# Loading the first expert's weights into the lower half of their slot instead of through three shared buffers

## The chip, the core and the metric

The kernel runs on one core of one Trainium2 chip. The metric is the device time of one execution in microseconds. The kernel before takes 1584.69 us, the median of three runs (1584.22 to 1586.04).

## What is computed

Three layers follow each other. An attention without a score matrix (softmax over the features of q, softmax over the sequence of k, products of k and v per head) gives 4608 rows of 512 features. Each row goes through one of eight experts (the one with the largest router value), and the result of that layer through the two best of eight other experts, chosen with noise. Cut to what matters:

```
q_s = softmax(q, features);  k_s = softmax(k, sequence)      # 8 batches, 8 heads, 576 x 64
x   = q_s @ (k_s^T @ v)                                      # 4608 x 512

# layer 1, one expert per row
e   = argmax(x @ w_gate);  g = softmax(x @ w_gate)[e]
x2  = g * (relu(x @ w1[e]) @ w2[e])                          # w1: 512 x 1024, w2: 1024 x 512

# layer 2, two experts per row
noisy = x2 @ w_gate2 + log1p(exp(x2 @ w_noise)) * noise
out   = sum over the top two: softmax weight * (relu(x2 @ w1'[e]) @ w2'[e])
```

## The kernel before

Rows are routed to experts in lists, and an expert's rows are worked off in blocks of 128. A block multiplies its rows by w1 and w2 of its expert. To keep float32 precision TensorE multiplies in three products: each operand x is split into a high part, hi = x rounded to TensorE's reduced float32 type, and a low part, lo = x - hi; a product is hi*hi + lo*hi + hi*lo.

One expert's weights fill a *slot* of on-chip memory: 16384 float32 columns on 128 partitions, the hi parts in columns 0 to 8191 and the lo parts in columns 8192 to 16383. Two slots lie side by side in a hand-placed tensor `W` (line 1694), declared in the reduced type. While the first stage runs, the second slot's bytes hold the attention's inputs, through a second hand-placed tensor `A` (line 1696). Because W and A share memory, the code declares with `apart` (line 168) that instructions on the first slot ("W0") and on A don't depend on each other.

The program has a first stage, and then loops over blocks. The first stage is one list of steps (class `Plan`): each step names its engine, a cost, what it reads and writes, and a lag after which its result can be used. A list scheduler orders these steps by the length of what still hangs on them, tries several settings, keeps the order with the shortest planned end, and issues the instructions of every engine in that order. On the chip each engine, and the SyncE queue (SP) that issues nearly all transfers, works its instructions strictly in that order, and waits where a dependency found by the framework is not yet met. The stage holds:

- the attention over eight batches and 36 tiles of 128 rows (`query`, line 1455): load q (SP), maximum (VectorE), transposes (TensorE), exponential (ACT), product (TensorE), copy to a row buffer `xrow` (ACT, line 1306), scaling (VectorE or GpSimd, line 1322), store to memory (SP, line 1327). There are five row buffers;
- the router of layer 1 in five groups of tiles (`gates`, line 1479): VectorE steps, two products on TensorE (lines 1393 and 1394), and one indirect store per tile by GpSimd that enters the rows in the lists (line 1420);
- the weights of the *first expert*, that of row 0, which is known after the first group (`first_parts`, line 810). They come in eight parts of 1024 columns, 512 KB each. Parts 0 to 3 hold w1, parts 4 to 7 hold w2. For each part there is a load by SP (line 151), a cast to the hi part by ACT (line 208) and a subtraction raw - hi by VectorE (line 215);
- two blocks of that expert (`first_blocks`, line 829), whose rows are gathered by GpSimd (line 271) and transposed by TensorE (line 257). The second half of a block's second product (`y1`) needs parts 6 and 7. The second block also runs the router of layer 2. During it the rows of the first loop block are gathered, for which all lists must be complete.

The eight parts pass through three buffers, in the order (1, 0, 2, 1, 0, 2, 0, 2): buffer 0 is `raw0`, buffer 1 is `h`, where the blocks keep their hidden values, and buffer 2 lies in `x2`, where they keep results. A load into a buffer waits until cast and subtraction of the part before it in that buffer are done. For the plan the buffers are named ("raw", 0) to ("raw", 2); the activations that write `h` and `x2r`, and a store of zero rows from `x2r` (line 1745), name them too.

Of the kernel before, what the change touches and what calls it, by code (L numbers as in the profile page):

```python
# [10 lines left out]
F32 = mybir.dt.float32  # L11
# [11 lines left out]
N, D, E, F = B * S, H * HD, 8, 1024  # L23
# [6 lines left out]
K = 4  # L30
SL = 8192 // K
HL = SL // 2
SLOT = 16384
# [114 lines left out]
def load_part(nc, z, raw, i, c0=0, n=SL):  # L148

    a = z.wall[i] if isinstance(i, int) else z.wall[ds(i, 1)].rearrange("o p x -> (o p) x")  # L150
    return nc.sync.dma_start(raw, a[:, c0:c0 + n])
# [25 lines left out]
class Parts:  # L177

    def __init__(self, nc, z, i, ahi, alo, halves, raws, mm=None, apo=None):
        self.nc, self.z, self.i, self.ahi, self.alo, self.apo, self.mm = nc, z, i, ahi, alo, apo, mm
        self.to_load, self.halves, self.raws = list(halves), list(halves), list(raws)
        self.use, self.his, self.los = {}, {}, []

    def load(self, n):
        for _ in range(min(n, len(self.to_load))):
            k = self.to_load.pop(0)
            self.use[k] = self.raws.pop(0)
            load_part(self.nc, self.z, self.use[k], self.i + k // 2, k % 2 * HL, HL)  # L190

    def free(self, i, others, late):
        for y in others:
# [18 lines left out]
    def lo(self, k, pool=False):  # L212
        z = self.z
        eng, o = (self.nc.gpsimd, self.apo) if pool else (self.nc.vector, self.alo)
        i = eng.tensor_tensor(cols(z, o + 8192 + k * HL, HL), self.use[k], f32(cols(z, o + k * HL, HL)),
                              op=OP.subtract)
        self.free(i, [h for n, h in self.his.items() if n != k] + [y for y in self.los if y.ins.engine != i.ins.engine],
                  self.late(k))
        self.los.append(i)
        self.raws.append(self.use.pop(k))  # L220

    def go(self, n):
        for _ in range(n):
# [586 lines left out]
def first_parts(nc, z, P, regs):  # L810

    add, parts = P.add, []
    seq = (1, 0, 2, 1, 0, 2, 0, 2)
    raws = [(z.raws[0], z.h, z.x2[:, 0:HL])[i] for i in seq]

    def load():
        if not parts:
            parts.append(Parts(nc, z, regs[0] * K, 0, 0, range(2 * K), raws, apo=0))
        parts[0].load(1)

    for k in range(2 * K):
        raw = ("raw", seq[k])
        add("SP", 1.46, load, ["expert"], [raw, "parts' turn"], 1.0)
        add("ACT", 0.95, lambda k=k: parts[0].hi(k), [raw], [("hi", k)])
        pool = k in POOL_LO
        add("POOL" if pool else "DVE", 2.0 if pool else 1.14, lambda k=k, pool=pool: parts[0].lo(k, pool), [raw, ("hi", k)], [("lo", k), "parts' end"])


def first_blocks(tc, z, pipe, P, wreg, late):
# [21 lines left out]
    def block(i):  # L851
        b = bs[i]
        mm(b.m0, 4, ["xhi"] + W("hi", 0, 1, 2, 3), "pk")
        mm(b.m0, 8, ["xhi", "xlo"] + W("lo", 0, 1, 2, 3), "pk")
        if i:
            gate(0)
        add("ACT", 0.48, lambda: b.relu(0), ["pk"], ["h0", ("raw", 1)])
        mm(b.m1, 4, ["xhi"] + W("hi", 0, 1, 2, 3), "pkv")
        mm(b.m1, 4, ["xlo"], "pkv")
        if i:  # L860
            gate(1)
        add("PE", 0.44, lambda: b.turn(0), ["h0"], ["px0"], 0.25)
        add("ACT", 0.48, lambda: b.hi(0), ["px0"], ["hhi0"])
        add("DVE", 0.6, lambda: b.lo(0), ["px0", "hhi0"], ["hlo0"])
        mm(b.m1, 4, ["xhi"] + W("lo", 0, 1, 2, 3), "pkv", end if i else None)
        add("ACT", 0.48, lambda: b.relu(1), ["pkv"], ["h1", ("raw", 1)])
        if i:
            gate(2)
        mm(b.y0, 4, ["hhi0"] + W("hi", 4, 5), "pq", end if i else None)
        mm(b.y0, 4, ["hlo0"], "pq", end if i else None)  # L870
        add("PE", 0.44, lambda: b.turn(1), ["h1"], ["px0"], 0.25)
        add("ACT", 0.48, lambda: b.hi(1), ["px0"], ["hhi1"])
        add("DVE", 0.6, lambda: b.lo(1), ["px0", "hhi1"], ["hlo1"])
        mm(b.y0, 4, ["hhi0"] + W("lo", 4, 5), "pq", end if i else None)
        if i:
            gate(3)
            table1()
        mm(b.y1, 4, ["hhi1"] + W("hi", 6, 7), "pq", end if i else None)
        turn_in()
        mm(b.y1, 4, ["hhi1", "hlo1"] + W("lo", 6, 7), "pq", end if i else None)  # L880
        mm(b.y1, 4, ["hhi1", "hlo1"] + W("lo", 6, 7), "pq", end if i else None)
        if i:
            gate(4)
        add("ACT", 0.57, b.result, ["pq", "iB"], ["x2r", ("raw", 2)])

    def gate(i):
        if i == 0:
# [798 lines left out]
@with_exitstack  # L1686
def tile_kernel(ctx: ExitStack, tc: tile.TileContext, q, kT, v, wg, noise, wgn, wall, out):
    nc = tc.nc
    z = Net()
    z.tc = tc  # L1690
    z.wall, z.out, z.noise = wall, out, noise
    at = -(-nc._sbuf_addr_for_side("left") // 32) * 32
    nc.alloc_sbuf_tensor("room", [128, 2 * SLOT], F32)
    z.W = nc.alloc_sbuf_tensor_at("W", [128, 2 * SLOT], F32R, offset=at).ap()

    z.A = nc.alloc_sbuf_tensor_at("A", [128, SLOT], F32, offset=at + SLOT * 4).ap()
    cp = ctx.enter_context(tc.tile_pool(name="const", bufs=1))
    z.tabs = cp
    dr = ctx.enter_context(tc.tile_pool(name="dram", bufs=1, space=bass.MemoryType.DRAM))
    ctx.enter_context(tc.manual_schedule())  # L1700

    z.xg = dr.tile([N + 128, D], F32, name="xg")
    z.lists = dr.tile([2 * E * CAP + 256 * (MAXB + 6), LW], I32, name="lists")
    nc.scalar.preload_act_table_set(ACT_SET)
    z.wgn = cp.tile([128, 4, 16], F32, name="wgns")
    z.w3 = cp.tile([128, 4, 3, 16], BF16, name="w3")
    z.sp0 = cp.tile([1, 1], F32, name="sp0")
    z.spacer = cp.tile([128, 2], I32, name="spacer")
    z.wgs = cp.tile([128, 4, 8], F32, name="wgs")
    early_pool(tc, z, cp)  # L1710
    wp = ctx.enter_context(tc.tile_pool(name="late", bufs=1))
    z.before_rows, z.sent = [], None
    late_pool(z, wp)
    consts(tc, z, cp)
    nc.vector.memset(z.yo, 0.0)
    banks(z, ctx.enter_context(tc.tile_pool(name="ps", bufs=1, space=PSUM)))
    SPE = [ET.SP]

    with ExitStack() as pctx:
        pipe = Pipe(tc, z, pctx, q, kT, v, noise)  # L1720
        P = Plan()
        add = P.add
        add("SP", 0.05, lambda: nc.sync.dma_start(z.wgs, wg.rearrange("(c p) e -> p c e", p=128)), (), ["wgs"], 2.0)
        add("POOL", 0.44, lambda: lists_iota(tc, z, cp), (), ["la"])
        add("DVE", 0.4, lambda: lists_pads(nc, z), (), ["la"])
        add("SP", 1.68, lambda: fill_lists(nc, z, 0), ["la"], ["lists0"], 2.0)

        def early():
            add("PE", 0.33, lambda: early_counts(nc, z, pipe.cum, pipe.first), ["cum", "first"], ["sm"], 0.25)
            add("DVE", 0.87, lambda: early_rows(nc, z, pipe.g1), ["sm"], ["taken"])  # L1730
            add("SP", 0.3, lambda: regs.extend(load_regs(nc, pipe.firsti, [0], 7, [ET.SP])), ["first"], ["expert"])
            add("SP", 0.3, lambda: regs.extend(load_regs(nc, z.takeni, [0], 256, [ET.SP])), ["taken", "expert"], ["takenr"])

            add("SP", 0.64, lists, ["takenr"] + [("lists", gi, u) for gi in range(EARLY) for u in range(GROUPS[gi])],
                ["li0", "li1", "lists0"], 3.1)

        regs = []

        def lists():
            for i in range(2):  # L1740
                load_list(nc, z, z.li[i], regs[0] * CAP + i * 128)

        add("PE", 3.5, lambda: warm_up(nc, z), (), ["pq"])
        pipe.plan(P, early)
        add("SP", 0.73, lambda: nc.sync.dma_start(z.xg[N:N + 128, :], z.x2r[:, 0:512]), [("raw", 2)], ())
        first_parts(nc, z, P, regs)
        add("SP", 0.05, lambda: nc.sync.dma_start(z.wgn, wgn), (), ["wgn"], 2.0)
        add("DVE", 0.9, lambda: weight_parts(nc, z), ["wgn"], ["xr"])
        T1, ce, sr, parts = first_blocks(tc, z, pipe, P, regs, ctx)
    xp = ctx.enter_context(tc.tile_pool(name="gate16", bufs=1, side="right"))  # L1750
    z.x3 = [xp.tile([128, 512], BF16, name=f"x3{i}") for i in range(3)]
    z.h32, z.hT = z.x2[:, 0:F], xp.tile([128, F], F32, name="hT")
    moe1(tc, z, T1, ce, z.tab1, 0)
    T2, ce2 = between(tc, z, sr, parts)
    moe2(tc, z, T2, ce2, z.tab2, sr)
# [32 lines left out]
```

## Time and profile before

| | |
|---|---|
| median of three runs | 1584.69 us (1584.22 to 1586.04) |
| the profiled execution | 1587.33 us |
| its span, first to last instruction | 1585.1 us |
| mean granted TensorE clock | 0.991 of full speed |
| TensorE busy (matmuls) | 1535.5 us, 97% |
| VectorE, ACT, GpSimd busy | 1066.9, 859.8 and 553.4 us |
| transfers | 296.50 MB, mean 187 GB/s |

The times below the table's second line come from one profiled execution; its span leaves out what lies before the first and after the last instruction. In the views, PE is TensorE, PEld its weight loads, DVE is VectorE, POOL is GpSimd, SPq the queue in which SyncE issues transfers. L243 is line 243 of the kernel. In a timeline row, the bracket gives the idle time of the engine before the row and what ended it.

### The profile page before, as it was taken

To read this page: it belongs to the slowest core of one execution; us is meant where nothing else is said; L and a number is where in the kernel's file an instruction comes from. 1 tells how busy PE (TensorE), PEld (TensorE's weight loads), DVE (VectorE), ACT (ScalarE), POOL (GpSimd) and SP (SyncE) were. 2 spreads that over 40 slices of the span, in tenths; PEclk is the share of its full clock that TensorE was granted. 3 is DMA by queue.
4 is the path that set the end of the run, shared out by engine and by line. 5 is a ranking of instruction groups with operands and counts; after the bars stand their busy time and mean duration, and the time that the engine had idled before them with its cause. 6 is when DMAs were issued, how large, how long until landed. Compare 5 with 4: busy or idle time off the path is not lost.

```text
span 1585.1 us, 43825 instructions
## 1 busy us (share of the span) xinstructions
PE 1535.5 (97%) x8222; PEld 1220.8 (77%) x8222; DVE 1066.9 (67%) x2894; ACT 859.8 (54%) x1895; POOL 553.4 (35%) x617
## 2 busy tenths in 40 slices
PE   8988899999999999988999999999999999999997
PEld 7867677777777777766788888888887888878885
DVE  6888677777777777765666666666666666666665
ACT  7766355555555555553555555555555555555554
POOL 4566444444444444442222222222222222222121
PEclk9999999999999999999999999999999999999998
DMA  9897544334334433423777778887777778777777
GB/s 328 270 286 221 188 140 138 125 136 136 123 134 140 140 136 125 138 94 94 208 209 213 208 211 212 208 217 209 215 206 203 218 207 214 211 203 216 205 213 185
DMA packets 194591, 296.50 MB, mean 187 GB/s; under 512 B 42560, under 2 KB 120896, under 8 KB 194560
## 3 DMA queue, kind: packets, MB, share of 16 engines
q1 hardware_dynamic: 166160, 234.63, 46.4%
q0 software_dynamic: 28400, 61.50, 19.0%
q8 instruction: 15, 0.25, 0.1%
q14 instruction: 16, 0.13, 0.0%
HBM read 185.53 MB, written 51.78 MB: 150 GB/s over the span
## 4 chain that ended last, share of the span: by engine, by line
PE 50%; DMA 2%; DVE 1%; SPq 1%; issue 1%; ACT 0%; POOLq 0%; ACTq 0%; DVEq 0%
PE pq L243 25%; PE pk L243 12%; PE pkv L243 12%; DMA out<-yo,meta 1%; DMA hT<-x 0%; SPq L529 0%; DMA raw<-raw 0%; ACT W L208 0%; SPq L463 0%; DMA xr<-xg,li 0%; DMA li<-lists 0%; DVE g_ns L355 0%; POOLq L1784 0%; SPq L474 0%; DVE x L524 0%
## 5 line engine op out<-in xcount | busy, mean ns | idle before, releaser
L243 PE MATMUL pq<-W,hhi 128*128 (+1 forms) x1840 | 499.8, 400 | 4.3 <-ACT W L208 3.5
L243 PEld LDWEIGHTS pq<-W,hhi 128*128 128x128 f32 x1840 | 339.1, 188 | 83.0 <-ACT W L208 3.9
L271 POOL DMA_INDIRECT xr<-xg,meta x113 | 119.5, 1057 | 522.4 <-DVE x L524 445.5
L164 DVE TENSOR_TENSOR W<-raw,W 128x1024 f32 x224 | 274.6, 1226 | 39.4 <-ACT touch L159 34.2
L243 PE MATMUL pq<-W,hlo 128*128 (+1 forms) x920 | 272.1, 408 | 0.6
L243 PE MATMUL pk<-W,xhi 128*128 (+1 forms) x928 | 255.6, 396 | 3.4 <-ACT x L967 2.0
L243 PE MATMUL pkv<-W,xhi 128*128 (+1 forms) x928 | 254.5, 395 | 0.0
L158 ACT CAST W<-raw 128x1024 f32 x224 | 231.7, 1034 | 0.0
L243 PEld LDWEIGHTS pk<-W,xhi 128*128 128x128 f32 x928 | 173.7, 188 | 47.3 <-issue 4.1
L243 PEld LDWEIGHTS pkv<-W,xhi 128*128 128x128 f32 x928 | 173.8, 188 | 43.4 <-issue 0.2
L535 ACT CAST hhi<-hT 128x512 fp32r<-128x512 f32 x148 | 84.4, 617 | 226.0 <-PE pkv L243 142.3
L243 PEld LDWEIGHTS pq<-W,hlo 128*128 128x128 f32 x920 | 163.9, 189 | 49.6 <-DVE hlo L512 16.0
L430 POOL DMA_INDIRECT out<-yo,meta x76 | 120.5, 1586 | 186.8 <-issue 184.1
L460 DVE STREAM_TRANSPOSE raw<-xr 128x512 f32<-128x512 f32 x74 | 81.6, 1102 | 117.0 <-DMA xr<-xg,meta 70.4
L540 DVE TENSOR_TENSOR hlo<-hT,hhi 128x512 fp32r<-128x512 f32 x148 | 95.8, 689 | 77.6 <-ACT hhi L535 77.6
L243 PE MATMUL pk<-W,xlo 128*128 (+1 forms) x464 | 137.9, 405 | 0.0
L243 PE MATMUL pkv<-W,xlo 128*128 (+1 forms) x464 | 137.8, 404 | 0.0
L469 ACT CAST xhi<-raw 128x512 fp32r<-128x512 f32 x74 | 46.0, 621 | 150.5 <-DMA raw<-raw 120.9
L410 POOL DMA_INDIRECT lists<-tl,g_di x78 | 109.2, 1400 | 36.6 <-issue 32.7
L524 DVE STREAM_TRANSPOSE x<-h 128x512 f32<-128x512 f32 x150 | 106.2, 708 | 4.9 <-ACT h L520 4.9
L243 PEld LDWEIGHTS pk<-W,xlo 128*128 128x128 f32 x464 | 84.9, 190 | 18.8 <-issue 0.2
L243 PEld LDWEIGHTS pkv<-W,xlo 128*128 128x128 f32 x464 | 84.0, 188 | 17.7
(309 smaller groups left out, 1935.2 us busy)
## 6 DMA issues: line engine op xcount, KB each, us to landing
raw<-in_wall SPq DMA_DIRECT2D x235, 512.0 KB
hT<-x SPq DMA_DIRECT2D x300, 128.0 KB
raw<-raw SPq DMA_DIRECT2D x296, 64.0 KB
out<-yo SPq DMA_DIRECT2D x40, 256.0 KB
A<-in_q SPq DMA_DIRECT2D x36, 256.0 KB
xg<-xrow SPq DMA_DIRECT2D x36, 256.0 KB
A<-in_v SPq DMA_DIRECT2D x8, 1024.0 KB
A<-in_kT SPq DMA_DIRECT2D x6, 1152.0 KB
```

The lines of the kernel that those rows point to most:

```text
L158: no_mm(z, nc.scalar.copy(cols(z, off + h * HL, HL), raw), h)
L164: no_mm(z, nc.vector.tensor_sub(cols(z, off + 8192 + h * HL, HL), raw, f32(cols(z, off + h * HL, HL))), h)
L243: i = z.tc.nc.tensor.matmul(self.out, lhsT=a, rhs=cols(z, self.wo + c, 512), start=self.start and self.n == 0, stop=self.stop and self.n = ...
L271: return nc.gpsimd.indirect_dma_start(out=z.xr, out_offset=None, in_=z.xg[0:n, :] if n else z.xg, in_offset=bass.IndirectOffsetOnAxis(ap=c ...
L410: i = nc.gpsimd.indirect_dma_start(out=z.lists, out_offset=bass.IndirectOffsetOnAxis(ap=t["di"][:, k:k + 1], axis=0), in_=z.tl[:, k, :], i ...
L430: nc.gpsimd.indirect_dma_start(out=z.out, out_offset=bass.IndirectOffsetOnAxis(ap=col(z, z.iB, 0), axis=0), in_=z.yo, in_offset=None, comp ...
L460: nc.vector.transpose(out=z.x32.rearrange("p (c k t) -> p c k t", c=4, k=4), in_=z.xr.rearrange("p (k j c) -> p c k j", k=4, c=4))
L469: nc.scalar.copy(hi, x)
L524: self.nc.vector.transpose(out=to, in_=self.z.h[:, i * 512:(i + 1) * 512].rearrange("p (c x) -> p c x", c=4))
L535: self.nc.scalar.copy(self.z.hhi[i].rearrange("p k (q t) -> p k q t", q=4), self.part32(i))
L540: self.nc.vector.tensor_sub(x, self.part32(i), f32(y))
```

## The change

The eight parts of the first expert are loaded into the columns of the slot where their lo parts will stand, columns 8192 to 16383. This place is written through a new hand-placed float32 tensor `R` over the first slot's bytes. The cast reads a part there and writes the hi part, and the subtraction then reads and overwrites the part in its place. The three buffers and their names leave the plan: a load now reads "expert" alone and writes the name of the lo part; the activations and the store of zero rows no longer name buffers. Each load is declared apart from the instructions on A. `Parts` is also used for the last weights of the stage, with buffers as before.

```diff
     def __init__(self, nc, z, i, ahi, alo, halves, raws, mm=None, apo=None):
-        self.to_load, self.halves, self.raws = list(halves), list(halves), list(raws)
+        self.to_load, self.halves, self.raws = list(halves), list(halves), raws and list(raws)

     def load(self, n):
         for _ in range(min(n, len(self.to_load))):
             k = self.to_load.pop(0)
-            self.use[k] = self.raws.pop(0)
-            load_part(self.nc, self.z, self.use[k], self.i + k // 2, k % 2 * HL, HL)
+            self.use[k] = self.raws.pop(0) if self.raws else self.z.R[:, self.alo + 8192 + k * HL:self.alo + 8192 + (k + 1) * HL]
+            i = load_part(self.nc, self.z, self.use[k], self.i + k // 2, k % 2 * HL, HL)
+            if not self.raws:
+                apart(self.z, "W0", i)
...
         self.los.append(i)
-        self.raws.append(self.use.pop(k))
+        if self.raws is not None:
+            self.raws.append(self.use.pop(k))
...
 def first_parts(nc, z, P, regs):
     add, parts = P.add, []
-    seq = (1, 0, 2, 1, 0, 2, 0, 2)
-    raws = [(z.raws[0], z.h, z.x2[:, 0:HL])[i] for i in seq]
     def load():
         if not parts:
-            parts.append(Parts(nc, z, regs[0] * K, 0, 0, range(2 * K), raws, apo=0))
+            parts.append(Parts(nc, z, regs[0] * K, 0, 0, range(2 * K), None, apo=0))
         parts[0].load(1)
     for k in range(2 * K):
-        raw = ("raw", seq[k])
-        add("SP", 1.46, load, ["expert"], [raw, "parts' turn"], 1.0)
-        add("ACT", 0.95, lambda k=k: parts[0].hi(k), [raw], [("hi", k)])
+        add("SP", 1.46, load, ["expert"], [("lo", k), "parts' turn"], 1.0)
+        add("ACT", 0.95, lambda k=k: parts[0].hi(k), [("lo", k)], [("hi", k)])
         pool = k in POOL_LO
-        add("POOL" if pool else "DVE", ..., [raw, ("hi", k)], [("lo", k), "parts' end"])
+        add("POOL" if pool else "DVE", ..., [("hi", k)], [("lo", k), "parts' end"])
...
-        add("ACT", 0.48, lambda: b.relu(0), ["pk"], ["h0", ("raw", 1)])
+        add("ACT", 0.48, lambda: b.relu(0), ["pk"], ["h0"])
-        add("ACT", 0.48, lambda: b.relu(1), ["pkv"], ["h1", ("raw", 1)])
+        add("ACT", 0.48, lambda: b.relu(1), ["pkv"], ["h1"])
-        add("ACT", 0.57, b.result, ["pq", "iB"], ["x2r", ("raw", 2)])
+        add("ACT", 0.57, b.result, ["pq", "iB"], ["x2r"])
...
+    z.R = nc.alloc_sbuf_tensor_at("R", [128, SLOT], F32, offset=at).ap()
     z.A = nc.alloc_sbuf_tensor_at("A", [128, SLOT], F32, offset=at + SLOT * 4).ap()
...
-        add("SP", 0.73, lambda: nc.sync.dma_start(z.xg[N:N + 128, :], z.x2r[:, 0:512]), [("raw", 2)], ())
+        add("SP", 0.73, lambda: nc.sync.dma_start(z.xg[N:N + 128, :], z.x2r[:, 0:512]), ["x2r"], ())
```

## Rows read from the trace of the kernel before

**Rows 1.** The page: busy time of each engine, share of the span, instructions.
```profile
PE 1535.5 (97%) x8222; PEld 1220.8 (77%) x8222; DVE 1066.9 (67%) x2894; ACT 859.8 (54%) x1895; POOL 553.4 (35%) x617
```

**Rows 2.** Stretches of the span: its length, each engine's busy time, clock, transfers.
```profile
0.00:185.50 185.50, 158.13 (x1610) 133.96 (x1610) 146.27 (x399) 114.59 (x270) 102.39 (x155) 0.96 0.85 264
...
780.00:1363.00 583.00, 583.00 (x2496) 466.47 (x2495) 372.56 (x626) 304.28 (x624) 134.63 (x104) 1.00 0.79 211
```

**Rows 3.** TensorE's timeline: start, length in us, instruction, idle before and releaser.
```profile
117.06 1.11 PE L1216 MATMUL pk<-ident,A 128*128 128x128 f32 x4 [2.83 <-ACT ek L1222]
...
138.91 0.63 PE L257 MATMUL sm<-ident,xr 128*128 128x128 f32 x4 [0.93 <-DMA xr<-xg,li]
...
155.68 0.42 PE L1394 MATMUL px<-ct,ones 128*128 128x48 f32 x2 [0.31 <-issue]
...
165.50 1.22 PE L243 MATMUL pq<-W,hhi 128*128 128x512 f32 x2 [3.49 <-ACT W L208]
...
171.29 1.10 PE L243 MATMUL pk<-W,xhi 128*128 128x512 f32 x4
...
176.82 1.10 PE L243 MATMUL pq<-W,hlo 128*128 128x512 f32 x4
177.76 0.60 PE L257 MATMUL px<-ident,h 128*128 128x128 f32 x4
...
180.91 0.66 PE L257 MATMUL sm<-ident,xr 128*128 128x128 f32 x4
```

**Rows 4.** ACT's timeline.
```profile
115.93 0.58 ACT L1306 COPY xrow<-px 128x512 f32<-128x512 f32 x1 [3.34 <-DMA xg<-xrow]
...
149.09 1.05 ACT L208 CAST W<-raw 128x1024 fp32r<-128x1024 f32 x1 [2.28 <-DMA raw<-in_wall]
...
164.40 1.04 ACT L208 CAST W<-x 128x1024 fp32r<-128x1024 f32 x1 [4.11 <-DMA x<-in_wall]
```

**Rows 5.** SyncE's queue, its issues (L151 weight loads, L1327 row stores).
```profile
111.12 0.34 SPq L151 DMA_DIRECT2D h<-in_wall  x1
111.70 0.33 SPq L1327 DMA_DIRECT2D xg<-xrow  x1
...
129.55 0.34 SPq L151 DMA_DIRECT2D raw<-in_wall  x1
...
141.58 0.35 SPq L151 DMA_DIRECT2D raw<-in_wall  x1
...
157.46 0.34 SPq L151 DMA_DIRECT2D x<-in_wall  x1
```

**Rows 6.** VectorE's timeline.
```profile
150.29 0.22 DVE L1314 TENSOR_SCALAR RS<-G 128x24 f32<-128x24 f32 x1 [2.27 <-issue]
...
155.61 0.69 DVE L1322 TENSOR_TENSOR xrow<-xrow,RS 128x512 f32<-128x512 f32 x1
156.21 1.22 DVE L215 TENSOR_TENSOR W<-x,W 128x1024 fp32r<-128x1024 f32 x1
...
165.48 1.23 DVE L215 TENSOR_TENSOR W<-x,W 128x1024 fp32r<-128x1024 f32 x1 [2.69 <-ACT W L208]
...
172.87 0.69 DVE L287 COPY x<-px 128x512 f32<-128x512 f32 x1 [1.07 <-PE px L257]
```

**Rows 7.** Stretches of 5 us, columns as in rows 2.
```profile
115.00:120.00 5.00, 2.94 (x24) 2.50 (x24) 3.69 (x9) 3.04 (x6) 3.23 (x4) 0.62 1.00 336
...
165.00:170.00 5.00, 4.50 (x11) 3.53 (x12) 4.21 (x17) 0.45 (x1) 3.36 (x5) 0.50 0.94 366
```

**Rows 8.** GpSimd's timeline: gathers (L271) and a list entry (L1420).
```profile
134.31 0.98 POOL L271 DMA_INDIRECT xr<-xg,li  x1 [0.15 <-DVE RS L1314]
...
160.61 0.96 POOL L1420 DMA_INDIRECT lists<-tok,di  x1 [4.72 <-DVE o_eqs L1548]
...
174.71 0.98 POOL L271 DMA_INDIRECT xr<-xg,li  x1 [2.61 <-DVE b_k L1634]
```

**Rows 9.** SyncE's reading of the expert's number: durations in ns, start.
```profile
L1043 SPq TENSOR_LOAD <-firsti x1: 484/484/484, 61.6 to 61.6; - x1
```

More of the change, by code (lines that the diff above doesn't have):

```diff
@@ L812, in first_parts @@
     add, parts = P.add, []
-    seq = (1, 0, 2, 1, 0, 2, 0, 2)
-    raws = [(z.raws[0], z.h, z.x2[:, 0:HL])[i] for i in seq]
     def load():
         if not parts:
-            parts.append(Parts(nc, z, regs[0] * K, 0, 0, range(2 * K), raws, apo=0))
+            parts.append(Parts(nc, z, regs[0] * K, 0, 0, range(2 * K), None, apo=0))
         parts[0].load(1)
     for k in range(2 * K):
-        raw = ("raw", seq[k])
-        add("SP", 1.46, load, ["expert"], [raw, "parts' turn"], 1.0)
-        add("ACT", 0.95, lambda k=k: parts[0].hi(k), [raw], [("hi", k)])
+        add("SP", 1.46, load, ["expert"], [("lo", k), "parts' turn"], 1.0)
+        add("ACT", 0.95, lambda k=k: parts[0].hi(k), [("lo", k)], [("hi", k)])
         pool = k in POOL_LO
-        add("POOL" if pool else "DVE", 2.0 if pool else 1.14, lambda k=k, pool=pool: parts[0].lo(k, pool), [raw, ("hi", k)], [("lo", k), "parts' end"])
+        add("POOL" if pool else "DVE", 2.0 if pool else 1.14, lambda k=k, pool=pool: parts[0].lo(k, pool), [("hi", k)], [("lo", k), "parts' end"])
 def first_blocks(tc, z, pipe, P, wreg, late):
```

## The prediction

> **What bounds the kernel now.** I read the page's busy times first: TensorE is busy for 1535.5 of 1585.1 us, 97%, no other engine over 67% [rows 1]. Then the busy time by stages: in the steady loop from 780 to 1363 us TensorE is busy without a gap, 583.00 of 583.00, while in the first 185.5 us (attention, first router, first two expert blocks) it is busy for 158.13, so 27.4 us are idle there [rows 2]. The change touches only this first stage. Everything after it is the same list of matmuls over the same blocks, so a first stage that ends x us earlier shifts the rest by x. The rest of the working is about which wait ends last in the stage.
>
> For that I read TensorE's timeline backwards from the stage's end. The reader is to see one large hole: at 165.50 it had sat idle for 3.49 us, released by the line-208 cast, that is by the high half of a weight part [rows 3]. ACT's timeline says why: this cast began at 164.40 after 4.11 us of idling for a transfer, and an earlier one at 149.09 after 2.28 us [rows 4]. The transfer queue closes the chain: the last weight part was issued at 157.46 [rows 5], 0.03 us after the subtraction of part 5 ended on VectorE (156.21 + 1.22 = 157.43) [rows 6]. Parts 5 and 7 share a buffer, so part 7 could not be fetched earlier. This is the wait that the change is able to remove.
>
> **The change part by part.** The weight loads: eight before, eight after, 512 KB each, one issue each, so added issues cost 0. What goes is the three-buffer rotation: load 7 behind subtraction 5, loads 3 to 6 behind their predecessors, and load 2 behind the store of the zero rows. The first five loads went out between 111.12 and 129.55, one per 4.6 us; the last three took until 157.46 [rows 5]. At the pace of the first five, part 7 is issued at 111.12 + 7 x 4.6 = 143.4 and, with the 6.94 us from its issue (157.46) to its cast (164.40), is ready at 150.4. TensorE asks for it at 165.50 - 3.49 = 162.0. So the stall goes with 11 us to spare.
>
> Term 1, the stall: 3.49 us.
>
> Term 2, the clock behind it: in 165 to 170 us the granted clock was 0.50, the lower of the two levels (1.2 GHz), after that idle stretch [rows 7]. The 14 matmuls from 165.50 to 171.29 took 5.79 us; four at the full clock advance 0.94 us (176.82 to 177.76) [rows 3], so 14 take 3.29. Without the idling: 2.50 us back. TensorE's own chain gains 3.49 + 2.50 = 5.99 us.
>
> Term 3, what is late next. The second block needs rows of the loop's first block gathered before its transposes at 180.91 [rows 3]; they come through the last group of tokens: router on VectorE, list entries on GpSimd from 160.61, gather at 174.71 [rows 8]. This chain carries weight waits too. Its first step on VectorE was at 150.29 after 2.27 us idle [rows 6], behind the ACT cast that waited for part 6 [rows 4]; and the subtraction of part 5 stood between the row multiplication (155.61) and the list places, which otherwise wait for TensorE's products (155.68 + 0.42 = 156.10): 157.43 - 156.30, 1.1 us [rows 3, 6]. With the parts there early, both go: 2.27 + 1.1, about 3.3 us. Its slack: the first gather took 138.91 - 134.31 = 4.60 us from issue to the transposes that waited for it [rows 3, 8]; at that price the rows are there at 174.71 + 4.60 = 179.3, 1.6 us before they were used. So this chain follows by 3.3 + 1.6 = 4.9 us and no more. VectorE's routing of the first layer sits behind 2.69 us idle and a 1.23 us subtraction at 165.48, and at 172.87 it waits 1.07 us for TensorE again [rows 6]: 5.0 us, so it is no tighter.
>
> The sum is the smaller of 5.99 and 4.9: 4.9 us.
>
> Subtracting in place, from the address it writes, is not shown for this instruction. The nearest rows: an in-place multiplication of 512 columns 0.69 us, 1024 columns from a buffer 1.22 [rows 6]. Twice 0.69 is 1.38, so between 0 and 0.16 us each; eight of them 0 to 1.3, beside idle VectorE. I take 0. Casts: same eight, same shape, 0. Transfers into the slot instead of a buffer: same bytes and the same 128 rows; a gain or a loss is bounded by the two landings seen, 6.94 and 7.51 us (141.58 to 149.09) [rows 4, 5], 0.6 us, covered by the 11 spare. The store of the zero rows and the two activations that wrote those buffers lose a wait each: 0 on the path. The moved step is the loads: each now asks only for the expert's number, read at 61.6 us [rows 9], yet the first went out at 111.12, because the list planner prefers the stage's other loads and stores. Later loads only close up to it, so they come into the queue ahead of row stores and query loads.
>
> What that costs is bounded by a row: a store issued at 111.70, right behind load 0 (111.12) [rows 5], let ACT go only at 115.93 after 3.34 us of waiting [rows 4]; TensorE then idled 2.83 us [rows 3] and the clock of 115 to 120 fell to 0.62 with the transfer engines at 1.00 [rows 7]. So one more such meeting costs 2.83 + 0.38 x 5 = 4.7 us; none costs 0. I take 0, since the moved loads are parts 5 to 7 and the stores they now pass come after 130 us; the other end is a rival. The Trainium skill speaks against me here: "DMA: Bandwidth & Descriptors", section "Queues, rings and completion order", has each transfer engine take the descriptors of a queue in ring order, so a 512 KB load ahead of a store delays it. The row of 111.70 agrees with it; by the page every passed store would pay so, which is the second rival.
>
> **The forecast** is 4.9 us less: the profiled execution, span 1585.1 and 1587.33 in all, becomes 1580.2 and 1582.4; the median of the runs, 1584.69, lies 2.64 below the profiled one and becomes 1579.8. Smallest gain: VectorE's 2.69 us alone, 1582.0. Largest: TensorE's 5.99 and ACT's 2.28 us for part 6, 8.3, so 1576.4.
>
> **Rivals.** First, slower: the loads queue behind the work on the slot. They write the slot through a second name, R, over bytes that casts, subtractions and matmuls use as W. The code already has to declare (lines 168 to 174) that W's lower half and A, which don't even touch, are independent, which suggests that accesses under different names of shared memory are ordered as wholes. The change declares the loads independent of A's users alone. If so, a load waits for the cast before it, or a cast for the load issued before it; SyncE's queue stands, with row stores behind it. The distance of two loads is then landing and cast: 6.94 + 1.04 = 8.0 us by part 7, or 7.51 + 1.05 + 1.22 = 9.8 by part 6 with its subtraction [rows 4 to 6]. It decides from 6.6 us, today's mean distance, (157.46 - 111.12) / 7. Seven distances make part 7 later by 7 x 8.0 - 46.3 = 9.7 us, or by 22.3, and TensorE already waits for it. By the nearer row, 1594.4; at the far end 1607. For it: the missing declarations. Against: no row of before has a second name for such bytes, so nothing shows the ordering.
>
> Second, nothing gained: the earlier loads meet stores in a full queue once more, 4.7 us, at the place of 115.93. It decides from a second store that lands 4.2 us late (111.70 to 115.93). 1584.69 - 4.9 + 4.7 = 1584.5. For it: transfer share 1.00 there. Against: that stretch already holds loads 0 and 1.
>
> Third, the change doesn't do it: the planner leaves part 7 behind the last stores, since free buffers did not bring load 0 forward from 61.6 either. The cast still waits: 1584.7.
>
> **Chances.** Forecast 0.48, loads ordered behind the slot's work 0.39, full queue 0.07, late order 0.06. About 0.2%, 3.2 us, is what a measurement here tells from no change. Of the forecast 0.44 is beyond that and 0.04 within; of the ordered loads 0.37 is slower and 0.02 within; the other two are within but for 0.01 slower. Faster 0.44, same 0.18, slower 0.38. The forecast's own range is 1576.4 to 1582.0. The whole one runs from 1576.5 to 1602: below it 0.04 of the forecast, above it 0.15 of the ordered loads.
>
> **What would show it.** Right: the eight weight loads within some 35 us in the transfer queue, no cast of line 208 released late by a transfer, no idle TensorE before the second half of block 0, full clock from 160 to 172, and the first loop block some 5 us before 185.5. Term 3 is right if the transposes for the loop's first block wait for the gather. Wrong: SyncE waiting for a line-208 cast or a subtraction before a weight load, or casts waiting for loads of other parts; then the first rival holds. A longer ACT wait for row stores shows the second, a weight load after 150 us the third.

## The result and the profile after

The change made the kernel slower: 1598.78 us (1595.09 to 1600.5, six runs) against 1584.86 (1584.22 to 1586.04, six runs) for the kernel before. The ratio is 1.0084, with a 95% interval of 1.0072 to 1.0097. The profiled execution took 1596.76 us, its span is 1594.9.

The busy times of the page look alike [rows 1]; only the idle time grew.

```profile
PE 1537.0 (96%) x8222; PEld 1225.4 (77%) x8222; DVE 1064.3 (67%) x2894; ACT 859.4 (54%) x1895; POOL 550.0 (34%) x617
```

Stretches of the span after, columns as in [rows 2].

```profile
0.00:185.50 185.50, 150.23 (x1557) 129.18 (x1558) 136.69 (x337) 110.26 (x260) 97.32 (x152) 0.93 0.80 256
...
780.00:1363.00 583.00, 583.00 (x2499) 467.35 (x2499) 371.69 (x624) 304.45 (x624) 135.10 (x105) 1.00 0.79 211
...
135.00:140.00 5.00, 1.02 (x5) 1.02 (x6) 2.99 (x6) 1.04 (x1) 2.62 (x6) 0.50 0.80 230
...
155.00:160.00 5.00, 0.00 (x0) 0.00 (x0) 1.77 (x6) 2.15 (x4) 2.25 (x5) 0.69 0.41 99
160.00:165.00 5.00, 3.59 (x12) 3.23 (x13) 2.45 (x2) 2.60 (x4) 4.21 (x8) 0.50 0.51 169
```

The loop is untouched, 583.00 of 583.00. The first 185.5 us have 150.23 us of TensorE instead of 158.13 [rows 2]. From 155 to 160 us TensorE does nothing at all, and the granted clock behind both holes is 0.50, the lower level. TensorE's timeline shows the two holes and the loop's entry.

```profile
138.98 1.12 PE L1245 MATMUL sm<-ident,bd 128*128 128x128 f32 x4 [7.87 <-DVE bd L1240]
...
161.41 2.05 PE L247 MATMUL pk<-W,xhi 128*128 128x512 f32 x4 [7.33 <-DMA R<-in_wall]
...
196.98 1.28 PE L247 MATMUL pk<-W,xhi 128*128 x4 [1.72 <-ACT x L968]
```

The hole of 3.49 us at 165.50 [rows 3] is gone. In its place stand 7.87 and 7.33 us, 11.7 more in sum. The loop's first matmul starts at 196.98; in the profile before it started at 185.54, so the loop is entered 11.4 us later. (The whole span is 9.8 us longer; a single profile is uncertain by some 3 us, as e11 below shows.)

SyncE's queue says where the holes come from. First its timeline (weight loads alone), then in another fence the line's own summary, which gives the first and the last start and who waited for these transfers.

```profile
119.05 0.34 SPq L151 DMA_DIRECT2D R<-in_wall  x1
...
126.17 0.34 SPq L151 DMA_DIRECT2D R<-in_wall  x1
...
132.06 0.34 SPq L151 DMA_DIRECT2D R<-in_wall  x1
...
151.29 5.79 SPq L151 DMA_DIRECT2D R<-in_wall  x2
```

```profile
L151 SPq DMA_DIRECT2D R<-in_wall x8: 342/344/350, 107.3 to 156.7; - x8
...
who waited for it (us, times):
  ACT W L211: 17.6, 5
  DVE W L218: 15.4, 4
  PE pk L247: 7.3, 1
```

VectorE's and ACT's timelines, the subtractions (L218) and casts (L211) of the same parts:

```profile
124.83 1.23 DVE L218 TENSOR_TENSOR W<-R,W 128x1024 fp32r<-128x1024 f32 x1 [3.97 <-DMA R<-in_wall]
...
130.71 1.23 DVE L218 TENSOR_TENSOR W<-R,W 128x1024 fp32r<-128x1024 f32 x1
...
136.93 1.23 DVE L218 TENSOR_TENSOR W<-R,W 128x1024 fp32r<-128x1024 f32 x1 [2.93 <-DMA R<-in_wall]
...
150.04 1.22 DVE L218 TENSOR_TENSOR W<-R,W 128x1024 fp32r<-128x1024 f32 x1 [4.12 <-DMA R<-in_wall]
```

```profile
117.93 1.09 ACT L211 CAST W<-R 128x1024 fp32r<-128x1024 f32 x1
...
124.71 1.04 ACT L211 CAST W<-R 128x1024 fp32r<-128x1024 f32 x1 [2.69 <-DMA R<-in_wall]
...
161.36 1.04 ACT L211 CAST W<-R 128x1024 fp32r<-128x1024 f32 x1 [3.55 <-DMA R<-in_wall]
```

Read them in order of time. Part 0 is cast from 117.93 to 119.02, and load 1 goes out at 119.05. The subtraction of part 0 needs nothing but that cast, yet it stands until 124.83, 0.12 us after part 1's cast, and both are released by the same load. It ends at 126.06; load 2 goes out at 126.17. The pattern goes on: 130.71 + 1.23 = 131.94 and load 3 at 132.06; 150.04 + 1.22 = 151.26 and load 6 at 151.29. Each load waits for a cast or a subtraction that was issued before it, of a part one or two back, and the work issued next waits for this load. TensorE is caught too: at 161.41 it begins a product of the first block with w1, whose parts 0 to 3 were loaded long before, and what released it is a weight load, the last one, issued at 156.7. The mean distance of two loads is (156.7 - 107.35) / 7 = 7.05 us. The first of these distances, 11.7 us, holds the time until ACT came to part 0's cast; the other six average 6.3.

### The profile page after: what moved, and what is told of

Its sections match the earlier page's. It is cut to its first block, busy times and chain, and to the rows that moved or that the text cites. A ratio compares the mean times of both kernels' runs of the same rounds, so it can differ in the third digit from the quotient of the medians.

```text
span 1594.9 us, 43680 instructions
## 1 busy us (share of the span) xinstructions
PE 1537.0 (96%) x8222; PEld 1225.4 (77%) x8222; DVE 1064.3 (67%) x2894; ACT 859.4 (54%) x1895; POOL 550.0 (34%) x617
## 4 chain that ended last, share of the span: by engine, by line
PE 53%; DMA 1%; DVE 0%; issue 0%; ACT 0%; SPq 0%; POOLq 0%; ACTq 0%; DVEq 0%
PE pq L247 26%; PE pk L247 13%; PE pkv L247 13%; DMA out<-yo,meta 0%; DMA hT<-x 0%; DMA xr<-xg,li 0%; SPq L533 0%; DVE g_u L356 0%; POOLq L1787 0%; PE px L261 0%; ACT W L211 0%; PE px L1666 0%; ACT yo L548 0%; DVE hlo L516 0%; PE sm L261 0%
```

## Theories and experiments

Theory A: the framework orders every access through the name R against every access through the name W, as wholes, whichever columns are meant. (The framework is the software that finds dependencies between instructions.) Theory B: the scheduler's new order is what costs. Without the buffers the plan counts a part as arrived soon after its load, and puts casts and subtractions too early in the order of ACT and VectorE. The experiments share chips in three groups (the first four runs, the next four, the last three), and each ratio is to runs of the kernel before on the same chip; that kernel's median was 1586.26 us there, then 1580.71, then 1581.65. Line numbers shift by some 10 between the kernels.

**e1: the declarations that the change left out.** Each load is declared independent of casts, subtractions and matmuls of other parts already issued, and these of loads of other parts. The changed condition puts a side effect right: in the changed kernel one load of the stage's last weights, the one that takes their last free buffer, is declared apart from A as well.

```diff
 # load of part k
-    if not self.raws:
+    if self.apo == 0:                        # loads of the first expert only
         apart(self.z, "W0", i)
+        for y in self.z.w0:                  # earlier casts, subtractions, matmuls
+            self.z.tc.declare_no_dep(i.ins, y.ins, reason=...)
+        self.z.loads.append((k, i))
 # cast and subtraction of part k; matmuls of the first slot likewise, for every load
+    self.z.w0.append(i)
+    for n, y in self.z.loads:
+        if n != k:
+            self.z.tc.declare_no_dep(i.ins, y.ins, reason=...)
```

> The changed kernel, with the loads on one side and the casts, subtractions and first-block matmuls on the other declared independent wherever they touch different parts; plan and order of all engines as in the changed kernel. Theory A (the ordering between the names R and W costs the time): the loads no longer wait for casts, casts and subtractions wait for their own part alone, and the time falls from 1598.8 below that of before, 1576 to 1583 us, 1580 the value of the prediction's sum. Theory B (the new order of the plan costs it, the waits only show it): it stays within 3 us of the changed kernel, 1596 to 1601. Both in part: between 1584 and 1595.

Measured: 1.0018 [1.0003, 1.0034]. Most of the loss is gone, not all, which is the case "both in part"; theory A's gain did not come. TensorE, VectorE, ACT and SyncE (four timelines):

```profile
133.10 1.12 PE L1255 MATMUL sm<-ident,bd 128*128 128x128 f32 x4 [5.37 <-DVE bd L1250]
```

```profile
128.00 1.23 DVE L225 TENSOR_TENSOR W<-R,W 128x1024 fp32r<-128x1024 f32 x1
...
131.06 1.22 DVE L225 TENSOR_TENSOR W<-R,W 128x1024 fp32r<-128x1024 f32 x1
132.20 0.85 DVE L1250 TENSOR_TENSOR bd<-pkv,rk 64x256 f32<-64x256 f32 x2
```

```profile
133.03 1.05 ACT L218 CAST W<-R 128x1024 fp32r<-128x1024 f32 x1 [3.69 <-DMA R<-in_wall]
```

```profile
127.20 0.34 SPq L151 DMA_DIRECT2D R<-in_wall  x1
```

This hole is of another kind. It ends when VectorE has done the attention's step L1250 at 132.20, and VectorE was busy, not waiting: between the subtractions of parts 1 and 2 it did steps of layer 2's router weights, and L1250 came behind all of them. In the kernel before, the same step follows directly on part 1's subtraction:

```profile
128.30 1.23 DVE L215 TENSOR_TENSOR W<-raw,W 128x1024 fp32r<-128x1024 f32 x1
129.44 0.86 DVE L1239 TENSOR_TENSOR bd<-pkv,rk 64x256 f32<-64x256 f32 x2
```

So the new order itself costs TensorE time here. ACT loses some beside it: the load of part 3 went out at 127.20 and the cast waits for its own part until 133.03, 5.8 us; the plan has put the cast closer behind the load than that.

**e2 and e3: one half of the declarations each.** e2 keeps the lines at the load, e3 those at casts, subtractions and matmuls.

> Half of that declaration: only the loads are independent of casts, subtractions and matmuls issued before them; those still wait for every load issued before them. Theory A1 (the harm is SyncE's queue standing at a load): most of the loss goes, 1581 to 1586 us. Theory A2 (the harm is casts, subtractions and matmuls that wait for loads of other parts): most of it stays, 1590 to 1600. Theory B: 1596 to 1601.

> The other half: casts, subtractions and matmuls wait for no load but their own part's; a load still waits for those issued before it. Theory A1: the loads stay 7 us apart and most of the loss stays, 1590 to 1600 us. Theory A2: VectorE, ACT and TensorE no longer stand, most of the loss goes, 1581 to 1588. Theory B: 1596 to 1601.

Measured: e2 1.0029 [1.0013, 1.0046], e3 1.0044 [1.0028, 1.0060]. With neither half it was 1.0084, with both 1.0018. At 1584.69 us for the kernel before, the two ratios are 1589.3 and 1591.7 us: e2 lies between its two ranges, e3 in theory A1's. Each half alone helps; the ordering goes in both directions, as the timelines of after show. In e2's profile the loads go out from 108.2 to 145.1 us, but TensorE still stands 2.59 us for one; in e3's it stands for none, but the loads take from 107.4 to 152.7. The intervals overlap, so which half counts for more is not shown.

**e4 and e5: the order of before, with and without the declarations.** The plan names the three buffers again, so every engine works in the order of before, while the loads still go through R. e5 adds e1's lines.

```diff
-        add("SP", 1.46, load, ["expert"], [("lo", k), "parts' turn"], 1.0)
-        add("ACT", 0.95, lambda k=k: parts[0].hi(k), [("lo", k)], [("hi", k)])
+        raw = ("raw", seq[k])
+        add("SP", 1.46, load, ["expert"], [raw, "parts' turn"], 1.0)
+        add("ACT", 0.95, lambda k=k: parts[0].hi(k), [raw], [("hi", k)])
```

> The plan of before, buffers' names and all, so that every engine has its instructions in the order of before; only the place of the loads is that of the changed kernel, through R, with the ordering between the names. Theory A: slower than before like the changed kernel, 1594 to 1604 us. Theory B: like before, 1583 to 1587.

> The plan of before (the order of every engine as in before), loads through R, and loads, casts, subtractions and first-block matmuls of different parts declared independent. Theory A (ordering between names): the loss of the same order with that ordering (ratio 1.0081) goes entirely; part 7 is still issued behind the last stores, so no more than before is gained: ratio 0.998 to 1.001. If something else in the place or the name is slow (transfers into the slot, subtraction in place), it stays above 1.003.

Measured: e4 1.0081 [1.0053, 1.0108], e5 1.0000 [0.9986, 1.0014]. This pair tells the theories apart: in one order of instructions the missing declarations alone make the difference, as large as the whole loss. (The two ran on different chips, each beside the kernel before; their intervals lie far apart.) TensorE's timeline of e4, then of e5:

```profile
155.19 2.05 PE L247 MATMUL pk<-W,xhi 128*128 128x512 f32 x4 [6.09 <-DMA xg<-xrow]
...
175.09 2.08 PE L247 MATMUL pq<-W,hlo 128*128 128x512 f32 x4 [4.92 <-DMA R<-in_wall]
...
197.58 1.17 PE L247 MATMUL pk<-W,xhi 128*128 x4 [1.99 <-ACT x L970]
```

```profile
164.11 0.74 PE L254 MATMUL pq<-W,hhi 128*128 128x512 f32 x2 [2.90 <-ACT W L218]
...
183.22 1.94 PE L254 MATMUL pk<-W,xhi 128*128 x4 [1.83 <-ACT x L980]
```

(In e4's first row the releaser named is a row store; ACT, which a weight load released at 155.05, began within 0.14 us of it, so that hole may be a load's too.) e5 is the kernel before but for the place where parts are loaded and split, and part 7 is as late as there, though no buffer holds it any more. SyncE's timeline of e5:

```profile
141.95 13.88 SPq L1340 DMA_DIRECT2D xg<-xrow  x6
155.93 0.38 SPq L151 DMA_DIRECT2D raw<-in_wall  x1
156.54 0.34 SPq L151 DMA_DIRECT2D R<-in_wall  x1
```

In SyncE's order part 7 stands behind these row stores and one other load. With e5 at 1.0000, loading to the slot and subtracting in place cost nothing that can be measured.

**e6, e7 and e8: a later arrival in the plan.** e1, with the plan told that a part can be cast 2, 4 or 6 us later.

```diff
+        add(f"landing{k}", 6.0, lambda: None, [("lo", k)], [("in", k)], 0.0)
-        add("ACT", 0.95, lambda k=k: parts[0].hi(k), [("lo", k)], [("hi", k)])
+        add("ACT", 0.95, lambda k=k: parts[0].hi(k), [("in", k)], [("hi", k)])
```

> The freed kernel, with one change in the plan: a part counts as arrived 2.0 later than the plan has it, so that casts and subtractions stand later in the order of ACT and VectorE. Theory C (what the freed kernel, ratio 1.0018, still loses comes from casts and subtractions planned some 2.5 us after the load's issue, while parts land 5 to 7 us after it, so that ACT and VectorE stand with other work behind them): between the freed kernel and the next one, ratio 0.999 to 1.001. Theory D (the loads themselves, issued earlier, push query loads and row stores back): as the freed kernel or worse, 1.001 to 1.004.

> The same with 4.0. Theory C: the parts have landed when ACT and VectorE come to them; the stand at part 3 (5.37 us of idle TensorE) goes and the gain of the forecast comes out, ratio 0.996 to 0.999. Theory D: 1.001 to 1.005, since the planner now issues the loads still earlier.

> The same with 6.0, about what a landing takes in this stretch. Theory C: as with 4.0 or 1 to 2 us better, ratio 0.995 to 0.999. Theory D: worst of the three, 1.002 to 1.006.

Measured: 1.0001 [0.9986, 1.0017], 1.0013 [0.9998, 1.0029] and 0.9996 [0.9981, 1.0011]. In e8 no cast waits for a transfer any more, and no wait for part 7 is left. None of the three is distinguishable from the kernel before. Theory C's gain did not come: e6 lies in its range, e7 in theory D's, e8 in neither. The hole that the same step of VectorE ends is 2.65, 0.92 and 2.89 us long in the three profiles, instead of 5.37, though the ratios do not follow it. The three runs support theory B for e1's remaining 0.0018, but e1 ran on another chip and its interval overlaps those of e6, e7 and e8, so that share is likely, not shown.

**e9: only what the forecast wanted.** e5, with part 7 issued right behind part 6 and every other instruction in e5's place.

```diff
-        parts[0].load(1)
+        parts[0].load(n)              # n = 1, 1, 1, 1, 1, 1, 2, 0 for the eight steps
```

> The plan of before with freed loads through R (ratio 1.0000 in the run before this), and part 7 issued right behind part 6 instead of behind the last stores; every other instruction stands where it stood. It tests the forecast's sum by itself: TensorE's stall before the second half of block 0 goes, and if the sum (4.9 us) holds, the ratio is 0.996 to 0.998. If the other chain (router of the last group, list entries, gather) holds the stage's end where it was, the stall only moves there: 0.999 to 1.001.

Measured: 1.0001 [0.9988, 1.0015]. Part 7's wait is gone, yet nothing is gained. Timelines of e9: SyncE, ACT, TensorE, GpSimd.

```profile
138.29 1.25 SPq L151 DMA_DIRECT2D R<-in_wall  x2
141.85 14.68 SPq L1340 DMA_DIRECT2D xg<-xrow  x6
```

```profile
153.15 0.59 ACT L1319 COPY xrow<-px 128x512 f32<-128x512 f32 x1 [2.86 <-DMA xg<-xrow]
...
163.58 1.05 ACT L218 CAST W<-R 128x1024 fp32r<-128x1024 f32 x1
```

```profile
154.29 1.11 PE L271 MATMUL px<-ident,h 128*128 128x128 f32 x4 [6.17 <-ACT h L517]
```

```profile
164.00 0.96 POOL L1433 DMA_INDIRECT lists<-tok,di  x1 [10.00 <-DVE o_eqs L1561]
```

The cast of part 7 (163.58) waits for nothing now. But its 512 KB went out ahead of the stores of rows from 141.85 on; ACT's copy into a row buffer waits 2.86 us for such a store, the activation behind it comes late, TensorE stands for 6.17 us (2.61 at the same place in e5; 1.46 in the kernel before on e9's chip), and GpSimd gets its list entries at 164.00 (159.80 in e5, 160.61 before [rows 8]). The summary of the six stores of this stretch in e9 names the wait (asked for up to 142.2 us only, it still does: it is the first store, issued at 141.85). Below it stand ACT and TensorE in the timeline of e5, where the same copy waits for no store:

```profile
L1340 SPq DMA_DIRECT2D xg<-xrow x6: 319/319/332, 141.9 to 156.2; - x6
...
who waited for it (us, times):
  ACT xrow L1319: 2.9, 1
```

```profile
149.36 0.59 ACT L1319 COPY xrow<-px 128x512 f32<-128x512 f32 x1
...
150.50 0.66 PE L271 MATMUL px<-ident,h 128*128 128x128 f32 x4 [2.61 <-ACT h L517]
```

In e9 this store let the copy go only 153.15 - 141.85 = 11.3 us after its issue. In e5 the store at its place was issued at 141.95, and the copy began 7.4 us later without a wait.

**e10 and e11: e8 and the kernel before, timed again beside e9.**

> The same kernel as the one with 6.0 before, measured more often: ratio 0.9996 with an interval of 0.3% there. If its shorter first stage (loop entered at 181.75 in its profile, 185.54 in that of before) is real, 0.997 to 0.999; if it was chance, 0.999 to 1.001.

> The kernel before, unchanged, as a measure of what no change looks like on this chip: ratio 1.000, within 0.001 either way by any theory.

Measured: e10 0.9992 [0.9981, 1.0004], e11 0.9999 [0.9988, 1.0010]. e10 has the lowest ratio of all, still not clear of no change and in the range named for chance, so no version is shown to beat the kernel before. Its profile enters the loop at 179.38, but that execution, 1576.9 us, was the fastest of its twelve (median 1581.43); the kernel before, profiled again in e11, entered at 182.57 instead of 185.54. One profile's stage end is thus uncertain by 3 us, and the verdicts here go by the ratios.

## Why the prediction was wrong

**What bounds the kernel: right.** Only the first stage changed; the loop has 583.00 us of TensorE in both profiles.

**What held part 7: only half right.** The prediction put part 7's late issue down to the buffer that it shares with part 5. In e5 no buffer holds it, and it goes out at 156.54, behind the row stores in SyncE's order. In the kernel before, SyncE's queue was taken until 156.74 + 0.38 = 157.12 as well, so the buffer held part 7 from there to 157.46 at most, 0.3 us. What could bring it forward was another place in the plan. SyncE's timeline of before:

```profile
143.47 13.18 SPq L1327 DMA_DIRECT2D xg<-xrow  x6
156.74 0.38 SPq L151 DMA_DIRECT2D raw<-in_wall  x1
```

**The casts and the subtraction in place: right.** Casts take 1.04 to 1.09 us, subtractions 1.22 or 1.23, as before [rows 4, 6], and e5 is at 1.0000 [0.9986, 1.0014].

**The step that failed: "each now asks only for the expert's number".** From it came the pace of 4.6 us, part 7 ready at 150.4, and the sum. The loads asked for more: for the casts and subtractions issued before them, on other columns of the same bytes. Measured are 7.05 us from load to load, and e4 against e5 shows that this ordering alone costs 0.8%. The first rival named this mechanism. 7.05 lies above its point of decision, 6.6, but only through the first distance (the other six average 6.3), and below its row-made bounds of 8.0 and 9.8; it is the pair e4 and e5 that decides, not the distance.

**The first rival's own path was wrong as well.** It priced a late part 7. Part 7 was issued at 156.7, no later than before [rows 5], and cast at 162.89 instead of 164.40. The loss came from elsewhere: casts and subtractions wait for other parts' loads while attention and router work stands behind them in ACT's and VectorE's order, and TensorE's first product with w1 waited 7.33 us for a load that it doesn't read. So its 1594.4 to 1607 holds the 1598.78 by the right mechanism, but not by the right sum; that the size fits is luck.

**Terms 1 to 3 and the sum of 4.9 us: not there even with free loads.** 4.9 us less is a ratio of 0.9969. e9, which gives term 1 its condition and nothing else, has 1.0001 [0.9988, 1.0015], and e10 0.9992 [0.9981, 1.0004]; 0.9969 lies outside both. Term 1's wait did go in e9, and with it term 2's idle stretch before part 7's matmuls; what took their place is the next item. Nor is the clock a sure cost of such a wait (term 2): in e5 TensorE stands 2.90 us for part 7's cast, and the clock behind it stays at 1.00. In e9 it is low earlier, with the new hole: 0.83 from 140 to 160 us, where e5 has 1.00. Two stretches of e5, then one of e9:

```profile
140.00:160.00 20.00, 16.21 (x93) 13.55 (x92) 15.30 (x56) 8.79 (x19) 8.99 (x16) 1.00 0.79 208
160.00:170.00 10.00, 5.70 (x24) 4.00 (x23) 7.36 (x31) 1.73 (x2) 7.28 (x12) 1.00 0.87 333
```

```profile
140.00:160.00 20.00, 13.32 (x67) 10.87 (x67) 12.36 (x39) 7.96 (x17) 8.71 (x15) 0.83 0.81 222
```

**The pushed stores at 0: wrong in e9.** The prediction argued that the loads moved ahead only meet stores after 130 us and so cost nothing. That stretch was not free: a store behind part 7's load let ACT go 11.3 us after its issue, and TensorE's hole grew by 6.17 - 2.61 = 3.6 us against e5, by 6.17 - 1.46 = 4.7 against the kernel before on the same chip. The second rival's price was 4.7 us too, but at the place of 115.93 and with 1.9 us of it for the clock, so that the two figures are equal is chance. The rule of the Trainium skill that was weighed there ("DMA: Bandwidth & Descriptors", section "Queues, rings and completion order") agrees with e9's store; of the six stores behind the load this one alone was waited for. Had the ordering on the slot not come first, the second rival, nothing gained, would have been the better forecast: e9 is at 1.0001, e1 at 1.0018.

**What stays open.** Whether a load through W's own name would have been ordered by columns was not tried, so it is not shown that the second name is to blame. The code of the kernel before speaks against it: it declares casts and subtractions of different parts independent (line 194), although all of them use the name W. Why e8 and e10, with neither a late part nor a late cast, measure no more than 0.04 and 0.08% below the kernel before was not settled; waits for row stores remain there, one of ACT's copies waits 4.54 us in e8 and 3.20 us in e10.

## What to carry to other kernels

When a change lets transfers write bytes that other instructions use, under a second name above all, ask what the framework will order before you count any transfer as free: list every instruction that touches the bytes, and price the chain load, work, load. A declaration already in the code for two names that do not even touch is a strong hint, worth more than a missing example. And a transfer moved forward can delay those that it passes, as in e9: in a queue with 512 KB loads and row stores, compute the gain and the pushed stores in one sum.

## What was not expected

The same unchanged kernel had medians of 1580.7 to 1586.3 us on different chips, and single runs on one chip from 1579.9 to 1591.2. A gain of 4.9 us is smaller than that scatter, so it takes ratios on one chip over many runs to see it.
